# Linear attention with a gated feed-forward: the order of the last block's products and stores, the PSUM pool of kv, the engine of one copy, the place of two weight sums

## The chip, the cores and the metric

The kernel runs on one core of a Trainium2 chip. A core has TensorE (PE: matrix products from SBUF into PSUM, with its weight loads listed apart as PEld), VectorE (DVE), ScalarE (ACT), GpSimd (POOL) and SyncE (SP), each with its own instruction queue worked off in order, and 16 DMA engines that the queues hand transfers to. The metric is the device time of one execution in microseconds (us), as a median over runs.

## The reference, cut to what matters

```python
def _attn_ref(q, k, v):                      # q, k, v: (8 batches, 8 heads, 576 rows, 64)
    q_s = softmax of q over its 64 columns    # exp, then divided by the row's sum
    k_s = softmax of k over its 576 rows      # exp, then divided by the column's sum
    kv = np.einsum('bhsd,bhse->bhde', k_s, v)
    return np.einsum('bhsd,bhde->bhse', q_s, kv)

def _moe_ref(x, w_gate, w_val, w_out):       # x: 4608 x 512; w_gate, w_val: 512 x 1536; w_out: 1536 x 512
    g = x @ w_gate
    gelu = 0.5 * g * (1.0 + erf(g / sqrt(2)))
    return (gelu * (x @ w_val)) @ w_out
```

`x` is the attention output with the heads side by side. The two softmax lines are written in words here; the rest is the reference's. Inputs and output are float32.

## The kernel before, in words

Each batch of 576 rows is cut into 512 main rows (a block) and 64 remaining rows; the 64 remaining rows of all eight batches form a ninth block of 512. The blocks run in the order 0 to 6, then the ninth (called `b == B`), and last batch 7 (L489). Products are in float16 with sums in float32 in PSUM.

One block has these steps, for twelve slices `fi` of 128 hidden columns. `ffn_fi` (L434) makes the gate product `psg` and the value product `psv`, four matmuls each; `gate` (L428) applies Gelu on ACT (`gl`, three buffers) and multiplies on VectorE into `ht`. Blocks 0 and 1 begin with `ffn_first0` and `ffn_first`, which start the products before all four slices of `xt` are there. Block 0 multiplies plainly by `w_out`. All other blocks use `out_strassen` (L550): a Strassen-Winograd form with seven products (`product`, L536) of twelve matmuls of 256 columns each, in place of eight. It needs sums of the weights (`sum_w`, L510: `tw` 1 to 4, made once) and sums of `ht` (`sum_h`, L524: `sh` 1 and 2, `s4`, and one in place). Its PSUM tiles are psa, psb and psc; `snap` copies an intermediate sum to SBUF, `add` adds it to a later one and writes the output tile `yo`.

Attention of later batches rides in between. `exp` (L174) takes exponentials on ACT; `norm` (L218) sums rows of exp(q) on VectorE and multiplies on GpSimd; `unit_td` (L341) transposes exp(q) by one DMA; `unit_kv4` (L294) makes kv from exp(k) and v on TensorE (`pskv`) and divides on VectorE; `unit_x4` (L380) makes x: first the remaining rows (`psxr`, copied to `xtr`), then the main rows (`psx`, copied to `xt`), with one half of the copies on ACT and the other on VectorE. For batch 1, x is made by `unit_x` (L364), one slice of 128 columns at a time, and copied whole by the engine that is named.

What rides where is written out by hand in `plan` (L722 to L778): `at(block, FI, i, ...)` runs the listed steps behind slice i of the block, `at(block, NS, 2 or 4, ...)` behind products 6 and 7 of its Strassen form. The order within each engine's queue is exactly the program's order (`manual_schedule`). The plan's places that the change touches are L741 (third slice of x of batch 1), L754 to L756 (weight sums 2 and 4, and `make_s`, which allocates the `sh` tiles, behind slices 4 to 6 of block 1) and L778 (`unit_kv4` of the next-but-one batch behind `unit_x4`).

PSUM has eight banks. Six are a ring (`big`, L66): a tile takes the tag at the front, which goes to the back at once, or, if held, when it is let go. Two banks are the pool `ps_att`. `bank` (L78) chooses: with `spare` true a tile comes from the ring, else from `ps_att`. `psxr` always takes both banks of `ps_att`; `pskv` of `unit_kv4` takes one of them except after block 3, where `spare` is true. A tile's first matmul waits until the last reader of the bank's earlier tile is done.

The SBUF tiles `yo` hold 256 output rows each, two to a partition: `yo[0]` those of the first half of the block, `yo[1]` those of the second. `store` (L499) issues one DMA to the output; in the last block the rows of `yo[1]` are written in half-rows of 256 columns. In blocks 1 to 6 the products run in the order 1, 2, 5, 6, 3, 7, 4. In the ninth block and the last one (`late`, L589) product 2, which completes the left half of `yo[0]`, comes after product 7:

```python
        late = b == B or last
...
        if last:
            for t in range(2):
                store(nc.sync, yo[1][:, t, c[1]], b, 2 + t, 3 + t, 256, 512)
        if late:
            second()
            store_rows(b, 0, yo[0])
```

In the last block each of psa, psb and psc is two tiles of 128 rows, and product 4 runs by row halves: the first half is copied to `yo[1]` by ACT, the second by VectorE, each followed by its store on SP's queue.

Of the kernel before, what the change touches and what calls it, by code (L numbers as in the profile page):

```python
# [11 lines left out]
ACTF = mybir.ActivationFunctionType  # L12
ALU = mybir.AluOpType

_H_SCALE = 1024.0
# [3 lines left out]
def kernel(  # L19
# [10 lines left out]
    nc = tc.nc  # L30

    B, H, S, D = q.shape
# [33 lines left out]
    def big(shape, dt, name, hold=False):  # L66
        tag = ring.pop(0)
        t = ps_big.tile(shape, dt, name=name, tag=tag)
        if hold:
            held[id(t)] = (t, tag)  # L70
        else:
            ring.append(tag)
        return t

    def let_go(t):
        ring.append(held.pop(id(t))[1])
# [419 lines left out]
    def out_rows(b):  # L496
        return out[b * S:(b + 1) * S, :].rearrange("(m n) c -> m n c", n=NT)

    def store(eng, src, b, n0, n1, c0=0, c1=C):  # L499
        base = out_rows(b)[:, 1 + n0:1 + n1, c0:c1]  # L500
        (pm, nm), (pn, _), _ = base.ap
        last = [[1, (n1 - n0) * C]] if c1 - c0 == C else [[1, c1 - c0]]
        eng.dma_start(out=bass.AP(tensor=base.tensor, offset=base.offset,
                                  ap=[[pm, nm], [NM * pn, 2]] + last), in_=src)
# [31 lines left out]
    def product(i, ps, first, ts=(0, 1)):  # L536
        for j in range(NO):
            for t in ts:
                c0, c1 = slice(t * P, (t + 1) * P), slice(256 + t * P, 256 + (t + 1) * P)
                a = {1: ht[:, j, c0], 2: ht[:, NO + j, c0], 3: s4[:, j, c0], 4: ht[:, NO + j, c1],  # L540
                     5: sh[1][:, j, c0], 6: sh[2][:, j, c0], 7: ht[:, j, c1]}[i]
                w = {1: wo_sb[:, j, 0:256], 2: wo_sb[:, NO + j, 0:256],
                     3: wo_sb[:, NO + j, 256:512]}.get(i)
                if w is None:
                    w = tw[{4: 4, 5: 1, 6: 2, 7: 3}[i]][:, j]
                nc.tensor.matmul(ps[t], a, w, start=(first and j == 0 and (  # L546
                    t == ts[0] or ps[t].tensor is not ps[ts[0]].tensor)),
                                 stop=(j == NO - 1), skip_group_check=True)

    def out_strassen(b, last):  # L550
        yo = [yop.tile([P, 2, C], f32, name="yo", tag="yo") for _ in range(2)]
        c = (slice(0, 256), slice(256, 512))
        ps, tiles_ = {}, {}

        def get(nm):
            if last:
                tiles_[nm] = [big([P, 256], f32, "ps" + nm, True) for _ in range(2)]
                ps[nm] = [x for x in tiles_[nm]]
            else:
                tiles_[nm] = [big([P, 2, 256], f32, "ps" + nm, True)]  # L560
                ps[nm] = [tiles_[nm][0][:, t] for t in range(2)]

        def parts(nm):
            return [(0, ps[nm][0]), (1, ps[nm][1])] if last else [(slice(0, 2), tiles_[nm][0])]

        def snap(nm):
            sn = ffn.tile([P, 2, 256], f32, name="sn", tag="gl")
            for n, (t, src) in enumerate(parts(nm)):
                if n:
                    nc.scalar.activation(out=sn[:, t], in_=src, func=ACTF.Copy, scale=1.0 / _H_SCALE)  # L570
                else:
                    nc.vector.tensor_scalar(out=sn[:, t], in0=src, scalar1=1.0 / _H_SCALE,  # L572
                                            scalar2=None, op0=ALU.mult)
            return sn

        def add(nm, sn, half, col):
            for t, src in parts(nm):
                nc.vector.scalar_tensor_tensor(  # L578
                    out=yo[half][:, t, c[col]], in0=src, scalar=1.0 / _H_SCALE,
                    in1=sn[:, t], op0=ALU.mult, op1=ALU.add)  # L580

        def second():
            get("b")
            product(2, ps["b"], True)
            add("b", s1, 0, 0)
            for x in tiles_["b"]:
                let_go(x)

        late = b == B or last  # L589
        get("a")  # L590
        product(1, ps["a"], True)
        s1 = snap("a")
        if not late:
            second()
        sum_h(NO - 2, NO, (4,))
        get("c")
        product(5, ps["c"], True)
        if not late:
            sum_h(NO - 2, NO, (3,))
        s5 = snap("c")  # L600
        if late:
            sum_h(NO - 2, NO, (3,))
        product(6, ps["a"], False)
        s2 = snap("a")
        ride(b, NS, 2)
        product(3, ps["c"], False)
        add("c", s2, 0, 1)
        for x in tiles_["c"]:
            let_go(x)
        if not late:  # L610
            store_rows(b, 0, yo[0])
        product(7, ps["a"], False)
        add("a", s5, 1, 1)
        ride(b, NS, 4)
        if last:
            for t in range(2):
                store(nc.sync, yo[1][:, t, c[1]], b, 2 + t, 3 + t, 256, 512)
        if late:
            second()
            store_rows(b, 0, yo[0])  # L620
        for ts in ((0,), (1,)) if last else ((0, 1),):
            product(4, ps["a"], False, ts)
            if ts == (1,):
                nc.vector.tensor_scalar(out=yo[1][:, 1, c[0]], in0=ps["a"][1],  # L624
                                        scalar1=1.0 / _H_SCALE, scalar2=None, op0=ALU.mult)
            else:
                t, src = parts("a")[0]
                nc.scalar.activation(out=yo[1][:, t, c[0]], in_=src, func=ACTF.Copy,  # L628
                                     scale=1.0 / _H_SCALE)
            if last:  # L630
                store(nc.sync, yo[1][:, ts[0], c[0]], b, 2 + ts[0], 3 + ts[0], 0, 256)
        for x in tiles_["a"]:
            let_go(x)
        if not last:
            store_rows(b, 1, yo[1])

    def store_rows(b, half, yo):
        if b < B:
            store(nc.sync, yo.rearrange("p n c -> p (n c)"), b, 2 * half, 2 * half + 2)
            return  # L640
        for t in range(2):
            for j in range(2):
                o = 2 * (2 * half + t) + j
                nc.sync.dma_start(
                    out=out[o * S:(o + 1) * S, :].rearrange("(m n) c -> m n c", n=NT)[:, 0, :],
                    in_=yo[j * 64:(j + 1) * 64, t, :])
# [75 lines left out]
    FI, NS = 0, 1  # L722
    plan = {}

    def at(b, kind, i, *fns):
        plan.setdefault((b, kind, i), []).extend(fns)

    L = lambda f, *a: (lambda: f(*a))
# [9 lines left out]
       L(sum_w, 3, "pool"))  # L738
    at(0, NS, 7, L(exp, "q", 2))
    first1 = [[L(unit_t, 1, 1), L(unit_kv, 1, 1)],  # L740
              [L(unit_x, 1, 2, "act"), L(preload, ACTF.Gelu), L(norm, 2, 0, "pool")],  # L741
              [L(unit_x, 1, 3, "dve"), L(norm, 2, 1, "pool")]]

    def x_upper0():
# [5 lines left out]

    at(1, FI, 2, L(unit_trem, 1))
    at(1, FI, 3, L(norm, 2, 2, "pool"), L(load_batch, 3, ((q, "q"), (k, "k"))))
    at(1, FI, 4, L(exp, "k", 2, 0, 4), L(norm, 2, 3, "pool"), make_s)
    at(1, FI, 5, L(sum_w, 2), L(cast_v, 2, 0, H))  # L754
    at(1, FI, 6, L(sum_w, 4))
    at(1, FI, 8, L(exp, "k", 2, 4, 8), L(unit_td, 2))  # L756
    at(1, FI, 11, L(load_batch, 3, ((v, "v"),)), L(exp, "q", 3), L(exp, "k", 3), L(cast_v, 3, 0, H))
    at(1, NS, 2, L(unit_kv4, 2))
# [3 lines left out]
    for b in range(2, B):  # L762
        if b + 2 < B:
            at(b, FI, 0, L(load_batch, b + 2, ((v, "v"), (q, "q"), (k, "k"))))
            at(b, FI, NFI - 1, L(exp, "q", b + 2), L(exp, "k", b + 2), *([exp_rem0] if b == 2 else []))
            vcast = L(cast_v, b + 2, 0, H)
        if b + 1 < B:
            n = b + 1
            for hp in range(HP):
                at(b, FI, hp, L(norm_sum, n, hp), L(norm_mul, n, hp, "pool"))  # L770
            at(b, FI, 4, L(unit_td, n))
            if n + 1 < B:
                at(b, FI, 4, vcast)
            if n == 3:
                at(b, FI, 5, L(unit_kv4, n))
            at(b, NS, 4, L(unit_x4, n, ("act", "dve"), 0 if n == 4 else None))
            if n + 1 < B:
                at(b, NS, 4, L(unit_kv4, n + 1, n == 4))  # L778


    def ride(b, kind, i):
        for fn in plan.get((b, kind, i), []):
            fn()
# [62 lines left out]
```

## Time and profile before

| | us |
|---|---|
| median of 4 runs (306.85 to 307.12) | 307.02 |
| the profiled execution | 307.08 |
| its span, first to last instruction | 305.3 |
| TensorE busy (96% of the span) | 293.8 |
| VectorE busy (66%) | 201.6 |
| ACT busy (48%) | 145.9 |
| GpSimd busy (27%) | 81.6 |
| last matmul issued, its products ended | 301.15 |
| last output store issued | 301.8 |

The time of an execution is the span and 1.78 us around it. The profile has one row for each instruction or run of equal instructions; in the timeline's rows the columns are start and duration in us, engine, line of the kernel, operation, the tile written and the tiles read, their shapes, and how many instructions the row joins. In square brackets stands how long the engine had been idle ahead of it and, as far as semaphores show it, what ended the wait. SPq rows are DMA issues on SP's queue: their duration is the issuing, not the transfer. The chain of waits is followed back from the last instruction: at each step to what released it.

### The profile page before, as it was taken

The page shows a single profiled execution, that of the slowest core. Times are in us where ns is not written, and L with a number is a line of the kernel's source. Part 1 is how long each engine was busy: PE and PEld are TensorE (multiplying, and loading weights), DVE is VectorE, ACT ScalarE, POOL GpSimd, SP SyncE. Part 2 cuts the span into 40 slices and gives each one's busy share as a digit, 9 for nine tenths or more (in the row PEclk, how much of TensorE's full clock was granted, in tenths as well). Part 3 has the DMA queues.
Part 4 walks back from the last instruction along what each step waited for, and adds up shares of the span by engine and source line. Part 5 has one row for each costly group of instructions (what it writes and reads, how often), then busy time and mean ns, then how long its engine had stood idle before and what let it go on. Part 6 is the DMA issues. An engine that isn't in the chain of part 4 may idle for free.

```text
span 305.3 us, 5368 instructions
## 1 busy us (share of the span) xinstructions
PE 293.8 (96%) x2077; PEld 167.5 (55%) x2077; DVE 201.6 (66%) x390; ACT 145.9 (48%) x195; POOL 81.6 (27%) x85
## 2 busy tenths in 40 slices
PE   3999999998999999999999999999999999999994
PEld 1544445445744575448544854486447644764473
DVE  2944377868866875877677758674867536834672
ACT  4763477789352574346633853385331333123320
POOL 2667568763036001800081007200600000000000
PEclk9999999999999999999999999999999999999999
DMA  7999999995189115950597049603040300032003
GB/s 230 372 383 392 400 388 385 328 304 159 71 257 322 44 45 194 375 85 2 188 382 120 1 153 378 160 0 140 0 86 3 124 16 0 0 79 60 1 2 137
DMA packets 54761, 51.66 MB, mean 169 GB/s; under 512 B 18512, under 2 KB 50768, under 8 KB 54736
## 3 DMA queue, kind: packets, MB, share of 16 engines
q1 hardware_dynamic: 53152, 49.75, 51.4%
q10 hardware_dynamic: 1584, 1.57, 1.6%
q8 instruction: 16, 0.26, 0.3%
q14 instruction: 9, 0.07, 0.1%
HBM read 37.75 MB, written 9.44 MB: 155 GB/s over the span
## 4 chain that ended last, share of the span: by engine, by line
PE 73%; DVE 0%; ACT 0%; issue 0%
PE psg L425 24%; PE psv L425 24%; PE psa L546 14%; PE psc L546 6%; PE psb L546 3%; PE pskv L301 2%; PE psx L388 1%; PE psxr L388 0%; DVE yo L578 0%; ACT xt L156 0%; DVE yo L624 0%; ACT xtr L156 0%; PE psxr L398 0%
## 5 line engine op out<-in xcount | busy, mean ns | idle before, releaser
L431 DVE SCALAR_TENSOR_TENSOR ht<-psv,gl 128x512 f16<-128x512 f32 x108 | 73.7, 685 | 66.4 <-PE psv L425 46.8
L430 ACT ACTIVATE gl<-psg 128x512 f32<-128x512 f32 x108 | 63.2, 597 | 95.6 <-PE psg L425 95.2
L425 PE MATMUL psg<-xt,wg_sb 128*128 128x512 f16 x384 | 100.5, 379 | 0.2 <-ACT xt L156 0.2
L425 PE MATMUL psv<-xt,wv_sb 128*128 128x512 f16 x384 | 100.5, 379 | 0.0
L425 PEld LDWEIGHTS <-wv_sb 128*128 128x128 f16 x432 | 42.2, 98 | 51.2 <-issue 0.7
L425 PEld LDWEIGHTS <-wg_sb 128*128 128x128 f16 x432 | 42.1, 98 | 48.7
L215 POOL TENSOR_TENSOR eq<-eq,rrq 128x640 f16<-128x640 f16 (+1 forms) x27 | 34.4, 1274 | 119.8 <-issue 103.0
L546 PEld LDWEIGHTS <-ht 128*128 128x128 f16 x384 | 37.1, 98 | 7.6 <-issue 0.8
L196 DVE TENSOR_REDUCE rq<-eq 128x10 f32<-128x640 f16 x28 | 22.7, 810 | 3.0 <-ACT eq L178 3.0
L546 PE MATMUL psa<-tw,ht 128*128 128x256 f16 x192 | 23.6, 273 | 0.2 <-DVE yo L578 0.2
L154 POOL CAST v<-vt 128x640 f16<-128x640 f32 x26 | 19.2, 781 | 9.4 <-DMA vt<-in_v_dram 9.4
L178 ACT ACTIVATE ek<-kt 128x1280 f16<-128x1280 f32 (+1 forms) x11 | 19.1, 1746 | 3.4 <-DMA kt<-in_k_dram 3.4
L546 PEld LDWEIGHTS <-sh 128*128 128x128 f16 x192 | 18.8, 98 | 3.1 <-issue 0.9
L178 ACT ACTIVATE eq<-qt 128x2560 f16<-128x2560 f32 (+2 forms) x10 | 18.5, 1864 | 2.5 <-DMA qt<-in_q_dram 2.5
L628 ACT ACTIVATE yo<-psa 128x512 f32<-128x512 f32 (+1 forms) x8 | 4.6, 570 | 20.4 <-PE psa L546 20.4
L572 DVE TENSOR_SCALAR sn<-psa 128x512 f32<-128x512 f32 (+1 forms) x16 | 10.4, 653 | 3.8 <-PE psa L546 3.8
L156 ACT CAST xtr<-psxr 128x128 f16<-128x128 f32 (+1 forms) x8 | 2.1, 290 | 22.1 <-PE psxr L388 15.1
L546 PE MATMUL psa<-tw,sh 128*128 128x256 f16 x96 | 11.8, 272 | 0.7 <-DVE sn L572 0.7
L425 PE MATMUL psg<-xtr,wg_sb 128*128 128x512 f16 x48 | 12.3, 379 | 0.0
L425 PE MATMUL psv<-xtr,wv_sb 128*128 128x512 f16 x48 | 12.3, 379 | 0.0
L546 PE MATMUL psb<-wo_sb,ht 128*128 128x256 f16 x96 | 12.0, 273 | 0.2 <-DVE ht L431 0.2
L546 PE MATMUL psc<-wo_sb,s 128*128 128x256 f16 x96 | 11.8, 273 | 0.0
(86 smaller groups left out, 265.3 us busy)
## 6 DMA issues: line engine op xcount, KB each, us to landing
out_dram<-yo SPq DMA_DIRECT2D x15, 512.0 KB, 3.3
kt<-in_k_dram SPq DMA_DIRECT2D x7, 640.0 KB, 8.5
vt<-in_v_dram SPq DMA_DIRECT2D x7, 640.0 KB, 5.0
qt<-in_q_dram SPq DMA_DIRECT2D x7, 640.0 KB, 6.8
qt<-in_q_dram SPq DMA_DIRECT2D x8, 512.0 KB, 7.4
wost<-in_moe_w_out_dram SPq DMA_DIRECT2D x6, 512.0 KB, 7.9
kt<-in_k_dram SPq DMA_DIRECT2D x6, 512.0 KB, 9.7
vt<-in_v_dram SPq DMA_DIRECT2D x6, 512.0 KB, 5.6
```

The lines of the kernel that those rows point to most:

```text
L154: nc.gpsimd.tensor_copy(out=dst, in_=src)
L178: nc.scalar.activation(out=dst[:, n0:NC, h0 * D:h1 * D].rearrange(o, d=D, **({"t": 2} if b >= QUAD else {})), in_=heads(tiles[(nm, b)], b, ...
L196: nc.vector.reduce_sum(rq, e, axis=mybir.AxisListType.X)
L215: (nc.gpsimd if eng == "pool" else nc.vector).tensor_tensor(out=e, in0=e, in1=rrq.unsqueeze(-1).to_broadcast((P, n, 2, D)), op=ALU.mult)
L301: nc.tensor.matmul(ps[s * D:(s + 1) * D, hp, :], ek_b[b % 2][:, n, c0:c0 + D], v16_b[b % 2][:, n, 2 * hp + s, 0:VW], start=(n == 0), stop= ...
L388: nc.tensor.matmul(ps[s][64 * t:64 * t + 64], st[(b, "kv4")][r, hp, :], src[r], start=True, stop=True)
L425: nc.tensor.matmul(ps, w[:, ci, fi * P:(fi + 1) * P], xt[:, ci, :], start=(ci == 0), stop=(ci == HP - 1))
L430: nc.scalar.activation(out=gl, in_=psg, func=ACTF.Gelu)
L431: nc.vector.scalar_tensor_tensor(out=ht[:, fi, :], in0=psv, scalar=_H_SCALE, in1=gl, op0=ALU.mult, op1=ALU.mult)
L546: nc.tensor.matmul(ps[t], a, w, start=(first and j == 0 and (t == ts[0] or ps[t].tensor is not ps[ts[0]].tensor)), stop=(j == NO - 1), ski ...
L572: nc.vector.tensor_scalar(out=sn[:, t], in0=src, scalar1=1.0 / _H_SCALE, scalar2=None, op0=ALU.mult)
L628: nc.scalar.activation(out=yo[1][:, t, c[0]], in_=src, func=ACTF.Copy, scale=1.0 / _H_SCALE)
```

## The change

The last block takes the order of blocks 1 to 6 up to product 3, so that `yo[0]` is complete and its 512 KB are stored (SP) ahead of products 7 and 4. These two run by row halves in a new function `finish_last`; one 128 KB half-row store goes out on ACT's queue, and two stores (256 KB and 128 KB) on SP's queue follow. `unit_kv4` behind `unit_x4` always takes its bank from the ring: after blocks 2, 4 and 5 too, not only after 3. The copy of the third x slice of batch 1 goes from ACT to VectorE, ahead of a norm sum. Weight sums 2 and 4 both run behind slice 4 of block 1, ahead of `make_s`, and not behind slices 5 and 6.

```diff
@@ out_strassen
-        late = b == B or last
+        late = b == B
...
         if not late:
             store_rows(b, 0, yo[0])
+        if last:
+            finish_last(b, ps["a"], yo[1], s5)
+            return
         product(7, ps["a"], False)
         add("a", s5, 1, 1)
         ride(b, NS, 4)
-        if last:
-            for t in range(2):
-                store(nc.sync, yo[1][:, t, c[1]], b, 2 + t, 3 + t, 256, 512)
         if late:
             second()
             store_rows(b, 0, yo[0])
-        for ts in ((0,), (1,)) if last else ((0, 1),):
-            product(4, ps["a"], False, ts)
-            if ts == (1,):
-                nc.vector.tensor_scalar(out=yo[1][:, 1, c[0]], in0=ps["a"][1],
-                                        scalar1=1.0 / _H_SCALE, scalar2=None, op0=ALU.mult)
-            else:
-                t, src = parts("a")[0]
-                nc.scalar.activation(out=yo[1][:, t, c[0]], in_=src, func=ACTF.Copy,
-                                     scale=1.0 / _H_SCALE)
-            if last:
-                store(nc.sync, yo[1][:, ts[0], c[0]], b, 2 + ts[0], 3 + ts[0], 0, 256)
-        for x in tiles_["a"]:
-            let_go(x)
-        if not last:
-            store_rows(b, 1, yo[1])
+        product(4, ps["a"], False)
+        nc.scalar.activation(out=yo[1][:, :, c[0]], in_=tiles_["a"][0], func=ACTF.Copy,
+                             scale=1.0 / _H_SCALE)
+        let_go(tiles_["a"][0])
+        store_rows(b, 1, yo[1])
+
+    def finish_last(b, ps, yo, s5):
+        for t in range(2):
+            product(7, ps, False, (t,))
+            nc.vector.scalar_tensor_tensor(
+                out=yo[:, t, 256:], in0=ps[t], scalar=1.0 / _H_SCALE, in1=s5[:, t],
+                op0=ALU.mult, op1=ALU.add)
+        store(nc.scalar, yo[:, 1, 256:], b, 3, 4, 256, 512)
+        product(4, ps, False, (0,))
+        nc.scalar.activation(out=yo[:, 0, 0:256], in_=ps[0], func=ACTF.Copy, scale=1.0 / _H_SCALE)
+        store(nc.sync, yo[:, 0], b, 2, 3)
+        product(4, ps, False, (1,))
+        nc.vector.tensor_scalar(out=yo[:, 1, 0:256], in0=ps[1], scalar1=1.0 / _H_SCALE,
+                                scalar2=None, op0=ALU.mult)
+        store(nc.sync, yo[:, 1, 0:256], b, 3, 4, 0, 256)
@@ plan
-              [L(unit_x, 1, 2, "act"), L(preload, ACTF.Gelu), L(norm, 2, 0, "pool")],
+              [L(unit_x, 1, 2, "dve"), L(preload, ACTF.Gelu), L(norm, 2, 0, "pool")],
...
-    at(1, FI, 4, L(exp, "k", 2, 0, 4), L(norm, 2, 3, "pool"), make_s)
-    at(1, FI, 5, L(sum_w, 2), L(cast_v, 2, 0, H))
-    at(1, FI, 6, L(sum_w, 4))
+    at(1, FI, 4, L(exp, "k", 2, 0, 4), L(norm, 2, 3, "pool"), L(sum_w, 2), L(sum_w, 4), make_s)
+    at(1, FI, 5, L(cast_v, 2, 0, H))
...
-                at(b, NS, 4, L(unit_kv4, n + 1, n == 4))
+                at(b, NS, 4, L(unit_kv4, n + 1, True))
```

## The prediction

> **What bounds the kernel now.** I read the page's totals first, then the chain that ended last, then the timeline at the places that the diff touches.
>
> ```profile
> PE 293.8 (96%) x2077; PEld 167.5 (55%) x2077; DVE 201.6 (66%) x390; ACT 145.9 (48%) x195; POOL 81.6 (27%) x85
> ...
> PE 73%; DVE 0%; ACT 0%; issue 0%
> ```
>
> TensorE is busy for 96% of the span, and the chain hardly leaves it. So an edit is worth what it takes out of TensorE's few gaps, plus what it does to the tail, where TensorE has ended (301.15 us) and only stores are left. The granted clock is 1.000, so no throttle is to be gained or lost. I work on the profiled execution: 307.08 us, a span of 305.3 us and 1.78 us around it; it lies 0.06 us above the median of 307.02.
>
> **Part 1: kv in the large pool.** After batches 2, 4 and 5 the sums pskv of the next-but-one batch move from the small PSUM pool (two banks) to the ring of six. After batch 3 they are there already, so the trace has both forms. Timeline at the end of batch 2:
>
> ```profile
> 113.01 0.61 PE L388 MATMUL psx<-eqt,kv 64*64 64x512 f16 x8
> 113.22 0.27 ACT L156 CAST xtr<-psxr 128x128 f16<-128x128 f32 x1 [1.92 <-PE psxr L388]
> 113.44 1.07 ACT L156 CAST xt<-psx 128x512 f16<-128x512 f32 x2
> 113.64 0.28 DVE L158 CAST xtr<-psxr 128x128 f16<-128x128 f32 x1
> ...
> 114.04 0.74 PEld L301 LDWEIGHTS <-ek 128*64 128x64 f16 x40 [0.91 <-ACT xt L156]
> 114.07 0.82 PE L301 MATMUL pskv<-v,ek 128*64 128x65 f16 x40 [0.45 <-ACT xt L156]
> ```
>
> The profile blames ACT's xt copy. In the built program the wait is on VectorE's xtr copy (113.64 + 0.28 = 113.92), whose bank pskv takes over; VectorE is late because it adds psa first. Now the ends of batch 3 (large pool) and of batch 4 (small pool):
>
> ```profile
> 145.03 0.60 PE L388 MATMUL psx<-eqt,kv 64*64 64x512 f16 x6
> ...
> 145.56 0.82 PE L301 MATMUL pskv<-v,ek 128*64 128x65 f16 x40
> ```
>
> ```profile
> 176.40 0.60 PE L388 MATMUL psx<-eqt,kv 64*64 64x512 f16 x8
> ...
> 176.93 0.71 PEld L301 LDWEIGHTS <-ek 128*64 128x64 f16 x40 [0.41 <-ACT xtr L156]
> 176.93 0.82 PE L301 MATMUL pskv<-v,ek 128*64 128x65 f16 x40
> ```
>
> From the last run of psx to pskv it is 0.53 us in both, and 1.06 us in batch 2. After batch 4 pskv inherits the bank that ACT frees (176.61 + 0.27 = 176.88), just in time; batch 5 stands likewise (207.77 to 208.30). So the gain is **1.06 - 0.53 = 0.53 us once**, and nothing after 4 and 5. In the built program the new bank after batch 2 was last read by the add of psc (ended 112.41), so it is free. What is late next: TensorE reaches the next gate product at 115.61 instead of 116.14; its xt copies end at 115.12 on VectorE. Margin 0.49 us, so it holds. The bank's next user is the third gate product of the next batch (117.34 at the earliest); the kv product on VectorE that frees it ends at 115.66. Bounds: 0.40 to 0.55.
>
> **Part 2: third x of batch 1 on VectorE.**
>
> ```profile
> 52.36 0.57 ACT L156 CAST xt<-psx 128x512 f16<-128x512 f32 x1
> ...
> 52.97 0.38 PE L425 MATMUL psg<-xt,wg_sb 128*128 128x512 f16 x1 [0.22 <-ACT xt L156]
> ...
> 53.47 0.63 DVE L158 CAST xt<-psx 128x512 f16<-128x512 f32 x1
> ...
> 54.27 0.38 PE L425 MATMUL psg<-xt,wg_sb 128*128 128x512 f16 x1
> ```
>
> ACT copies the third x at 52.36, after a 2.34 us exponential. Its product started at 51.29 and VectorE is idle from 51.47 to 52.48, so there the copy runs from about 51.74 to 52.37, and the reduce behind it, which waits for the same exponential (52.45), is not delayed. TensorE can go on at 52.37 + 0.215 (the pitch of these products) = 52.585 instead of 52.97: 0.385. But six products later it needs the fourth x, still copied from 53.47 to 54.10 behind that reduce. With 0.05 us for the signal (as 76.30 to 76.35 below) the product of 54.27 can start at 54.15. So **0.12 us** is left; bounds 0 and 0.385.
>
> **Part 3: the two weight sums go before the sixth gate.** They cost 1.07 and 0.94 us of VectorE (64.08 and 65.67). Behind the last norm sum VectorE is idle from 60.95 to 63.47, waiting for ACT, so they end at 62.97, ahead of the ht product queued behind them. That makes VectorE earlier only until 70.38, where it again waits for ACT's tenth Gelu (0.97 us). That Gelu hangs on ACT's chain of table loads, not on VectorE, so the TensorE stall on the twelfth ht (0.53 + 0.25 us of waits at 73.91) stays. What they do meet is GpSimd:
>
> ```profile
> 73.84 3.10 POOL L154 CAST v<-vt 128x640 f16<-128x640 f32 x4 [8.11 <-DMA vt<-in_v_dram]
> 73.89 0.95 DVE L532 TENSOR_TENSOR sh<-ht 128x512 f16<-128x512 f16 x1
> ...
> 74.87 0.82 DVE L532 TENSOR_TENSOR sh<-sh,ht 128x512 f16<-128x512 f16 x1
> 75.62 0.68 DVE L572 TENSOR_SCALAR sn<-psa 128x512 f32<-128x512 f32 x1
> 76.35 1.47 PE L546 MATMUL psa<-tw,sh 128*128 128x256 f16 x12 [0.74 <-DVE sn L572]
> ```
>
> These two sums have a median of 0.425 us; beside the cast they lost 0.53 + 0.40 = 0.93 us, and TensorE waits 0.74 us at 76.35. The other way round, the fourth cast at 64.29, started during the weight sum of 64.08 to 65.15, took 1.44 us instead of 0.72. So the moved sums will hold back the norm product on GpSimd (61.10, 1.26 us) by up to about 0.95 us, the rest of the first sum. Behind it on SP's queue stand the transpose (62.38, 5.10 us, waits for that product) and then the load of v (67.58) that releases the cast of 73.84: all later by as much. The sh sums then run free, and product 6 may start up to 0.9 us sooner. But then the cast, from 74.8 to 77.9, meets the next pair (s and ht, at 76.0 and 76.4), which the copy of psc waits for. With 0.93 us lost there, product 3 starts at 78.2 to 78.4 against 78.50. Bounds: 0.3 lost (three sums hit) to 0.8 gained (none hit). I take **0.13**, near the lower half, because the cast is moved and not removed.
>
> The rule that speaks against this part is in the Trainium skill, SBUF — State Buffer, section "Who interferes with whom": a VectorE operation with two SBUF inputs and a GpSimd operation that reads SBUF exclude each other, and whichever starts first holds the port for its whole instruction. Taken strictly it would let the norm product in between the two sums, and VectorE's next ht would start some 0.8 us late; the rows of 64.29 and 73.89 agree with it, and by it part 3 would stand at its low end, 0.3 us lost, if it went on blocking each pair in turn. From the rows alone: that ht may start up to 1.6 us late before anything feels it (0.5 us of idle, then 1.1 us until the Gelu of 65.26 wants its buffer), so I charge nothing.
>
> **Part 4: the end.** TensorE has the same 84 products in the last block and ends at 301.15 as before. Product 2 moves up behind product 1 and needs the twelfth ht (292.78) only for its last two pairs; the two sums before product 3 end by about 296.2, product 3 starts at 297.06. Product 7 by halves ends its first half at 299.03; its add runs 299.24 to 299.62, just before product 4 wants the bank (299.68). Before:
>
> ```profile
> 298.91 3.59 SPq L503 DMA_DIRECT2D out_dram<-yo  x5
> ...
> 300.53 0.38 ACT L628 ACTIVATE yo<-psa 128x256 f32<-128x256 f32 x1 [4.20 <-PE psa L546]
> 301.19 0.42 DVE L624 TENSOR_SCALAR yo<-psa 128x256 f32<-128x256 f32 x1 [0.66 <-PE psa L546]
> ```
>
> The five stores go out at 298.91, 299.5, 300.55 (512 KB), 301.18 and 301.8; by the DMA view they land after 2.1, 2.1, 3.0, 2.7 and 2.4 us, the last at 304.2, and 1.1 us later the span ends. From 301.75 to 303.75 the DMA engines are full: that is what stretches 2.1 to 2.4. After: 512 KB leaves at 299.29 (adds end at 299.22) and is gone by 302. The half row block goes out on ACT's queue at 300.22; its issue holds ACT (issues there took 0.65 to 0.72 us at the kernel's start), so the copy queued behind it starts at 300.90 instead of 300.53 and ends at 301.28. SP waits for it: 256 KB at 301.35 to 301.92, the last 128 KB at 301.82 to 301.95. Landing after 2.1 to 2.4 us gives 303.92 to 304.35 against 304.2: between 0.28 gained and 0.15 lost. I take **0.10 gained**, because the queue is emptier. Cover gone would mean a longer issue on ACT; see rival C.
>
> **Sum.** 0.53 + 0.12 + 0.13 + 0.10 = 0.88 us: 307.08 - 0.88 = **306.2 us**, 0.29% faster. About 0.2%, 0.61 us, is what a measurement of this kernel can tell from no change.
>
> **Rivals.**
> A, *only kv pays*: fourth x, cast and stores take everything else back. For it: each of the other parts runs into a next wait named above. 307.08 - 0.53 = 306.55, no difference that counts.
> B, *the cast slips past both pairs of sums*: parts 1, 2 and 4 give 0.75, part 3 its full 0.8: 305.5. Against it: the cast lasts 3.1 us and the sums stand 2 us apart.
> C, *slower: the store on ACT holds the last copy*. With an issue of length i the last store leaves at 300.22 + i + 0.38 + 0.06 + 0.61. The longest issue of an output store in this trace is 1.60 us: the last store then leaves at 302.87 and lands 2.4 to 3.0 us later (3.0 is the longest of the five), 1.07 to 1.67 later than now. With nothing from parts 2 and 3: 307.08 - 0.53 + 1.07 to 1.67 = 307.6 to 308.2, say 307.9. The kernel is slower than before from about i = 1.2 on (301.27 + 1.2 + 2.25 = 304.72, 0.52 late). Against it: the last five stores took 0.54 to 0.67 to issue.
> D, *the kv gain doesn't come*: another bank's wait stands in its place, the rest as forecast: 306.73.
>
> **Chances.** Forecast 0.54, A 0.24, B 0.13, C 0.05, D 0.04. Faster by over 0.2%: forecast and B, with a little of A's upper edge, 0.68; within: 0.27; slower: 0.05. The range 305.4 to 306.8 leaves out C, some of B and the worst of parts 3 and 4.
>
> **What would show it.** Batch 2's pskv 0.53 us behind its psx run; the product now at 54.27 about 0.1 us earlier; the norm product of 61.10 longer or later, the cast of 73.84 later, and the sh sums at 0.42 us; the last store issued near 301.9 less what came before. It is wrong if the cast stays beside the sh sums, if batch 3's first gate product waits for xt, or if the issue on ACT takes over 1 us.

## The result, and the profile after

| | before | after |
|---|---|---|
| median, us | 307.11 (76 runs) | 306.63 (51 runs) |
| profiled execution, us | 307.08 | 306.62 |
| its span, us | 305.3 | 304.8 |
| TensorE's last product ends, us | 301.15 | 300.59 |

The ratio is 0.9981, with a 95% interval from 0.9974 to 0.9987. The kernel is faster by 0.48 us, 0.16% by the medians: the forecast sign, inside the forecast range, but about half of the 0.88 us that were forecast, and just inside the 0.2% that the prediction called no change that can be told, although the interval leaves out 1. Rival A (306.55, only kv pays) is the nearest case. (The 76 runs of before include its runs beside the change; the prediction knew only 307.02.)

The totals and the chain of the page of after, against those of before:

```profile
PE 293.4 (96%) x2077; PEld 167.3 (55%) x2077; DVE 203.7 (67%) x391; ACT 145.5 (48%) x194; POOL 82.5 (27%) x85
...
PE 73%; DVE 1%; issue 0%
```

The same 2077 products take TensorE the same time. VectorE is busy 2.1 us longer and GpSimd 0.9 us, though only one copy moved to VectorE (0.69 us). Part of the rest is instructions that take longer: the two weight sums alone are busy 2.89 us where they took 1.07 + 0.94.

**End of batch 2, kv.** Timeline of after:

```profile
112.95 0.60 PE L388 MATMUL psx<-eqt,kv 64*64 64x512 f16 x8
112.97 0.69 DVE L578 SCALAR_TENSOR_TENSOR yo<-psa,sn 128x512 f32<-128x512 f32 x1 [0.62 <-PE psa L546]
113.17 0.27 ACT L156 CAST xtr<-psxr 128x128 f16<-128x128 f32 x1 [1.92 <-PE psxr L388]
113.38 1.07 ACT L156 CAST xt<-psx 128x512 f16<-128x512 f32 x2
...
113.48 0.82 PE L301 MATMUL pskv<-v,ek 128*64 128x65 f16 x40
113.58 0.28 DVE L158 CAST xtr<-psxr 128x128 f16<-128x128 f32 x1
...
115.56 0.81 PE L425 MATMUL psg<-xt,wg_sb 128*128 128x512 f16 x3
```

pskv now starts 0.53 us behind psx, and no longer 1.06. It starts before VectorE's xtr copy (113.58), so that copy's bank is not what it waits for any more. TensorE was 0.06 us ahead of the trace of before when this stretch began (112.95 against 113.01) and is 0.58 ahead at the next gate product (115.56 against 116.14), which starts without a wait.

**Third x of batch 1:**

```profile
50.34 2.34 ACT L178 ACTIVATE eq<-qt 128x2560 f16<-128x2560 f32 x1 [0.98 <-DMA qt<-in_q_dram]
...
51.73 0.69 DVE L158 CAST xt<-psx 128x512 f16<-128x512 f32 x1 [0.24 <-PE psx L367]
...
52.71 0.82 DVE L196 TENSOR_REDUCE rq<-eq 128x10 f32<-128x640 f16 x1 [0.29 <-ACT eq L178]
...
53.70 0.63 DVE L158 CAST xt<-psx 128x512 f16<-128x512 f32 x1
...
54.38 0.38 PE L425 MATMUL psg<-xt,wg_sb 128*128 128x512 f16 x1 [0.31 <-DVE xt L158]
```

The third copy sits where it was forecast (51.74), and the wait has moved to the fourth x, as forecast. But that product starts at 54.38, later than the 54.27 of before. Read upwards: fourth copy, norm sum, and the exponential, which started at 50.34 where it had 50.11 in the trace of before, because the load of q that it waits for landed 0.23 us later.

**The weight sums and the cast.** First the norm product, the transpose and the load of v before:

```profile
61.10 1.26 POOL L215 TENSOR_TENSOR eq<-eq,rrq 128x640 f16<-128x640 f16 x1 [0.40 <-DVE rrq L198]
...
62.38 5.10 SPq L344 DMA_TRANSPOSE eqt<-eq  x1
...
67.58 1.29 SPq L134 DMA_DIRECT2D vt<-in_v_dram  x2
```

Then after: where the sums went, and where the cast of batch 3's v meets the sums of block 1:

```profile
61.02 2.89 DVE L515 TENSOR_TENSOR tw<-wo_sb,tw 128x1536 f16<-128x1536 f16 x2
61.21 1.89 POOL L215 TENSOR_TENSOR eq<-eq,rrq 128x640 f16<-128x640 f16 x1 [0.40 <-DVE rrq L198]
...
63.12 4.39 SPq L344 DMA_TRANSPOSE eqt<-eq  x1
63.84 1.87 DVE L431 SCALAR_TENSOR_TENSOR ht<-psv,gl 128x512 f16<-128x512 f32 x3
...
67.61 1.29 SPq L134 DMA_DIRECT2D vt<-in_v_dram  x2
```

```profile
74.00 0.42 DVE L532 TENSOR_TENSOR sh<-ht 128x512 f16<-128x512 f16 x1
...
74.04 3.16 POOL L154 CAST v<-vt 128x640 f16<-128x640 f32 x4 [7.29 <-DMA vt<-in_v_dram]
...
74.46 0.82 DVE L532 TENSOR_TENSOR sh<-sh,ht 128x512 f16<-128x512 f16 x1
...
75.94 1.47 PE L546 MATMUL psa<-tw,sh 128*128 128x256 f16 x12 [0.21 <-DVE sn L572]
...
76.58 0.89 DVE L532 TENSOR_TENSOR s<-ht,sh 128x512 f16<-128x512 f16 x1
...
78.46 0.70 PE L546 MATMUL psc<-wo_sb,s 128*128 128x256 f16 x5 [0.30 <-DVE sn L572]
```

The norm product takes 1.89 us instead of 1.26, and the transpose is issued 0.74 us later (63.12 against 62.38). But its issue takes 4.39 us instead of 5.10, and the load of v behind it starts at 67.61 against 67.58: the lateness ends on SP's queue. The cast is 0.20 us late and not 0.7, and only 0.03 of that come from the queue: from the load's issue to the cast it is 6.43 us instead of 6.26 (6.12 to 6.57 in the other traces that have the cast at this place). That is enough to let the first sh sum start ahead of it; product 6 is 0.41 us earlier, the sum s pays (0.89 us instead of 0.42), and product 3 comes at 78.46 against 78.50.

**The end:**

```profile
297.79 2.80 PE L546 MATMUL psa<-tw,ht 128*128 128x256 f16 x24
...
298.66 3.52 SPq L503 DMA_DIRECT2D out_dram<-yo  x3
299.30 0.42 DVE L630 SCALAR_TENSOR_TENSOR yo<-psa,sn 128x256 f32<-128x256 f32 x1 [0.23 <-PE psa L546]
299.75 0.60 ACTq L503 DMA_DIRECT2D out_dram<-yo  x1
300.56 0.38 ACT L635 ACTIVATE yo<-psa 128x256 f32<-128x256 f32 x1 [3.50 <-PE psa L546]
300.63 0.42 DVE L638 TENSOR_SCALAR yo<-psa 128x256 f32<-128x256 f32 x1 [0.91 <-PE psa L546]
```

SP's stores are issued at 298.66, 300.96 and 301.63; by the DMA view the last lands after 2.1 us, at about 303.7. From TensorE's end to the end of the profiled execution it was 307.08 - 301.15 = 5.93 us; it is 306.62 - 300.59 = 6.03. The new tail loses 0.10 us.

So the account of the change is: 0.06 us ahead before kv, 0.52 from kv, 0.02 given up after it, hence 0.56 at TensorE's end; less 0.10 in the tail is 0.46 = 307.08 - 306.62.

### The profile page after: what moved, and what is told of

The parts are those of the page before. It is cut to its first block, busy times and chain, and to the rows that moved or that the text cites. A ratio compares the mean times of both kernels' runs of the same rounds, so it can differ in the third digit from the quotient of the medians.

```text
span 304.8 us, 5370 instructions
## 1 busy us (share of the span) xinstructions
PE 293.4 (96%) x2077; PEld 167.3 (55%) x2077; DVE 203.7 (67%) x391; ACT 145.5 (48%) x194; POOL 82.5 (27%) x85
## 4 chain that ended last, share of the span: by engine, by line
PE 73%; DVE 1%; issue 0%
PE psg L425 24%; PE psv L425 24%; PE psa L546 13%; PE psc L546 6%; PE psb L546 3%; PE pskv L301 1%; PE psx L388 1%; DVE yo L578 0%; PE psxr L388 0%; DVE s L532 0%; DVE sn L572 0%; DVE yo L638 0%; DVE ht L532 0%; PE psxr L398 0%
## 5 line engine op out<-in xcount | busy, mean ns | idle before, releaser
L546 PE MATMUL psa<-wo_sb,ht 128*128 128x256 f16 x96 | 11.8, 273 | 0.0
```

What stands on the lines that cost most here:

```text
L546: nc.tensor.matmul(ps[t], a, w, start=(first and j == 0 and (t == ts[0] or ps[t].tensor is not ps[ts[0]].tensor)), stop=(j == NO - 1), ski ...
```

## The experiments

My theory after the result: kv pays its 0.53 us and nothing else does; the third x is worth its 0.12 but hidden by a late load; the place of the weight sums is worth nothing, because sums and cast collide wherever they stand; the store on ACT's queue costs what the new order of the tail gains. Rivals: the parts pay but the tail costs more than it seems; or the moved sums are what delays things.

| kernel | us | ratio to before, 95% |
|---|---|---|
| kv_only | 306.63 | 0.9978 (0.9969 to 0.9987) |
| all_but_kv | 307.30 | 0.9996 (0.9983 to 1.001) |
| old_tail | 306.52 | 0.9978 (0.9968 to 0.9987) |
| store_on_sp | 306.15 | 0.9963 (0.9951 to 0.9976) |
| x_on_act | 306.84 | 0.9984 (0.9975 to 0.9993) |
| sums_back | 306.65 | 0.9983 (0.9974 to 0.9992) |
| x4_first | 306.32 | 0.9972 (0.9961 to 0.9983) |
| v_late | 305.88 | 0.9957 (0.9943 to 0.9971) |
| x_only | 307.05 | 0.9996 (0.9988 to 1.0005) |
| three_mends | 305.03 | 0.9930 (0.9917 to 0.9944) |
| four_mends | 304.61 | 0.9915 (0.9901 to 0.9928) |
| before_again | 307.13 | one execution |

### kv alone, and everything but kv

kv_only is before with one line changed, all_but_kv is after with that line as it was:

```diff
-                at(b, NS, 4, L(unit_kv4, n + 1, n == 4))
+                at(b, NS, 4, L(unit_kv4, n + 1, True))
```

> The kernel before with the large pool for kv after blocks 2, 4 and 5, and nothing else of the change. Theory: the kv edit is the whole gain. pskv of block 2 starts 0.53 us behind its last run of psx, the span is 0.5 us shorter than before's 305.3, the time 306.6 us, ratio 0.9983, like the whole change. Rival (the gain is spread over the parts): 306.85 us, ratio 0.9991.

> The whole change except the kv edit (the pool choice is as before). Theory: nothing is left, 307.1 us, ratio 1.000 (between 0.9995 and 1.0005), the last block about 0.06 us earlier than before and the tail giving it back. Rival (the gain is spread): 306.8 us, ratio 0.999.

Measured: 306.63 and 307.30, each beside a before of 307.28. kv alone is worth 0.65 us by the medians; the rest together can't be told from nothing (0.9996, from 0.9983 to 1.001). In the trace of kv_only psx starts at 112.85 and pskv at 113.39 (0.54); in all_but_kv 112.90 and 113.96 (1.06). Rival A of the prediction, that only kv pays, holds for the whole.

### The tail: old order, and the store on SP

old_tail is after with the last block's code of before. store_on_sp is after with this:

```diff
-        store(nc.scalar, yo[:, 1, 256:], b, 3, 4, 256, 512)
+        store(nc.sync, yo[:, 1, 256:], b, 3, 4, 256, 512)
```

> The change with the last block as it was before. Theory: the new tail costs about 0.1 us, so this is 0.1 us faster than the whole change: 306.5 us, the last store issued 0.65 us after TensorE's end and landing 2.4 us later. Rival (the new tail pays because its DMA queue is emptier): 0.1 to 0.3 us slower than the whole change, 306.75 to 306.9 us.

> The change with the half-row store of the last block on SP's queue instead of ACT's. Theory: ACT is free for the last copy, which starts about 0.1 us after its product ends (0.6 us earlier against the last block's first product than in the change), the last store is issued 0.65 us or less after TensorE's end instead of 1.04 and still lands about 2.1 to 2.3 us later: 0.3 to 0.5 us faster than the change, 306.2 to 306.3 us. Rival (the transfers themselves set the end): the stores come closer together, the last one lands 2.5 us or more after its issue, and the time is the change's 306.6 us.

Measured: 306.52, as forecast, and 306.15, just below the forecast. The timeline of store_on_sp:

```profile
297.97 2.80 PE L546 MATMUL psa<-tw,ht 128*128 128x256 f16 x24
...
298.84 2.97 SPq L503 DMA_DIRECT2D out_dram<-yo  x4
299.48 0.42 DVE L630 SCALAR_TENSOR_TENSOR yo<-psa,sn 128x256 f32<-128x256 f32 x1 [0.23 <-PE psa L546]
300.15 0.38 ACT L635 ACTIVATE yo<-psa 128x256 f32<-128x256 f32 x1 [2.91 <-PE psa L546]
```

Its TensorE runs 0.18 us later than that of after (297.97 against 297.79), yet ACT's copy starts at 300.15 against 300.56: measured from TensorE, 0.59 us earlier. The last store goes out at 301.26 against 301.63, 0.55 us earlier by the same measure. What held ACT in after is its own queue. The view of line L635 of after (durations in ns as least, median and most, then the first and last start in us):

```profile
L635 ACTq EVENT_SEMAPHORE  x2: 38/38/38, 300.4 to 300.5; - x2
L635 ACT ACTIVATE yo<-psa x1: 383/383/383, 300.6 to 300.6; 128x256 f32<-128x256 f32 x1
```

The issue holds ACT from 299.75 to 300.35, two semaphore instructions follow, and the copy starts only at 300.56, though the views name psa as its releaser. So the new order is worth about 0.37 us against the old tail when SP issues all stores (306.15 against 306.52), and 0.11 us less than nothing when ACT issues one. The second difference is inside the intervals; the traces put it at 0.10 as well (from TensorE's end to the end of the execution 5.93 us in old_tail, 6.03 in after). In store_on_sp it is 5.48 us: the last store goes out 0.49 us after TensorE's end (0.65 before) and lands after 2.1 us (2.4 before). So the rival of store_on_sp, that the transfers set the end, is out. That the last 0.21 us (300.35 to 300.56) are those two waits is read from the rows, not tested by itself. The Trainium skill, DMA: Bandwidth & Descriptors, section "Issuing engines are not separate DMA queues", says that issuing from several engines saves only the sequencer's time for the issue, usually small beside the transfer; here that time, 0.60 us, was taken from the engine that had the critical copy behind it.

### Third x: back to ACT, alone, and the fourth x first

x_on_act is after with the third x on ACT again; x_only is before with the third x on VectorE; x4_first is after with the norm sum behind the fourth x:

```diff
-              [L(unit_x, 1, 2, "dve"), L(preload, ACTF.Gelu), L(norm, 2, 0, "pool")],
-              [L(unit_x, 1, 3, "dve"), L(norm, 2, 1, "pool")]]
+              [L(unit_x, 1, 2, "dve"), L(preload, ACTF.Gelu)],
+              [L(unit_x, 1, 3, "dve"), L(norm, 2, 0, "pool"), L(norm, 2, 1, "pool")]]
```

> The change with the third x of batch 1 copied on ACT again. Theory: the fourth x sets the end of this stretch in both forms (its copy stands behind a norm sum that waits for an exponential), so the product that needs it starts at 54.3 us here as at 54.38 in the change: 306.6 us, within 0.1 us of the change. Rival (the third x holds TensorE for 0.385 us): 307.0 us, the product at 54.7.

> The kernel before with the third x of batch 1 copied on VectorE, and nothing else. Theory: TensorE gains 0.12 us at the product that needs the fourth x, measured against the end of the exponential that the copy stands behind (which follows the load of q and was at 52.45 us in one trace of before and up to 52.69 in others): that product starts 1.70 us behind the exponential's end instead of 1.82; 307.1 us, within 0.15 of before. Rival (the copy itself is worth its 0.385 us): 306.8 us.

> The change with the norm sum of batch 2 moved behind the copy of the fourth x on VectorE. Theory: the fourth x is there at about 53.3 us, its product starts at 53.9 instead of 54.38, and TensorE is 0.45 us earlier up to product 6 of that block; there the cast of v takes part of it back, so 0.1 to 0.45 us faster: 306.2 to 306.5 us. Rival (the first Gelu waits for its table load, or the cast takes back all): 306.6 us.

> The kernel before once more, for a second trace. Theory: the start of the exponential of batch 2's q follows the load stream and varies by some 0.2 us from execution to execution of one kernel; here anywhere from 50.1 to 50.4. Rival (something in the change shifts it by 0.2 us): 50.1 again. The rest as in the first trace: span 305.2 to 305.5 us.

Measured: 306.84, 307.05 and 306.32. x_on_act is 0.21 us above after, where at most 0.1 was forecast; x_only is 0.14 below its before (307.19). That is the direction of the move, but not to be told from nothing by these intervals. The traces tell it, if the exponential's end is the zero point. To the product that needs the fourth x it is 1.70 us with the move (after 52.68 to 54.38; x_only 52.65 to 54.35) and 1.81 or 1.82 without (before 52.45 to 54.27; before_again 52.63 to 54.44; x_on_act 52.68 to 54.50). The move is worth **0.12 us**, as forecast. (In x_on_act's trace another 0.08 us go at the sums of block 1, see the table below.) The exponential itself starts at 50.11 in the first trace of before and at 50.29 in before_again, the same program; with the move it starts at 50.34 in after and at 50.11 in four_mends below. So the 0.23 us that hid the gain need no edit to explain them: on the page of after the DMA engines are full there (387 and 388 GB/s in the two slices from 38 to 53 us), and the load lands a little sooner or later from one execution to the next. Timeline of x4_first, the third and the fourth copy:

```profile
51.85 0.69 DVE L158 CAST xt<-psx 128x512 f16<-128x512 f32 x1 [0.24 <-PE psx L367]
...
52.93 0.69 DVE L158 CAST xt<-psx 128x512 f16<-128x512 f32 x1 [0.39 <-PE psx L367]
```

With the fourth copy ahead of the sum it no longer waits for the exponential: the product that needs it starts at 54.03 instead of 54.38, and the output products of block 2 start 0.35 us earlier than in after (104.56 against 104.91). That is the gain that the forecast saw at the third x (0.385) and lost at the fourth.

### The sums back, and the cast away

sums_back is after with the weight sums at their old places. v_late moves the load and the cast of batch 3's v behind the sums of block 1:

```diff
-    at(1, FI, 11, L(load_batch, 3, ((v, "v"),)), L(exp, "q", 3), L(exp, "k", 3), L(cast_v, 3, 0, H))
+    at(1, FI, 11, L(exp, "q", 3), L(exp, "k", 3))
...
-    at(1, NS, 4, L(unit_x4, 2, ("act", "dve"), 1))
+    at(1, NS, 4, L(unit_x4, 2, ("act", "dve"), 1), L(load_batch, 3, ((v, "v"),)), L(cast_v, 3, 0, H))
```

> The change with the two weight sums where they were before. Theory: their place is worth nothing, because SP's transpose issue gets shorter by what it starts later (4.4 instead of 5.1 us) and the load of v leaves at 67.6 us either way; whether the cast starts just ahead of the sh sums or just behind them is chance, and product 3 starts at 78.3 to 78.6 in all cases: 306.6 us, within 0.15 of the change. Rival (the place is what gained): the sh sums take 0.95 and 0.82 us again, product 3 starts 0.2 us or more later than 78.46, 306.8 us or more.

> The change with load and cast of batch 3's v put behind block 1's stores, so that GpSimd is idle while VectorE makes the last sums of block 1. Theory: the sums take 0.42 us each, product 6 starts at about 75.5 and product 3 at 77.5 to 77.7 instead of 78.46, and the cast, now at 87 to 91 us, is done before kv of batch 3 wants it at 93.8: 0.7 to 0.9 us faster, 305.75 to 305.95 us. Rival 1 (something else than GpSimd made these sums slow): the sums stay at 0.8 to 0.95 us and the time at 306.6. Rival 2 (the cast now meets block 2's norm products and kv of batch 3 waits for it): product 3 is early, kv of batch 3 late, 306.4 us or more.

Measured: 306.65 and 305.88. The same three places in each trace, as start of the cast, start of the first sh sum, length of the two sh sums and of s, and time from the start of the first sh sum to product 3 (us):

| kernel | cast | sh | sh, sh, s | to product 3 |
|---|---|---|---|---|
| before | 73.84 | 73.89 | 0.95, 0.82, 0.42 | 4.61 |
| before_again | 73.90 | 74.07 | 0.83, 0.82, 0.41 | 4.49 |
| kv_only | 73.69 | 73.92 | 0.76, 0.82, 0.41 | 4.43 |
| x_only | 74.18 | 73.98 | 0.42, 0.82, 0.89 | 4.46 |
| sums_back | 74.07 | 73.92 | 0.43, 0.82, 0.89 | 4.46 |
| after | 74.04 | 74.00 | 0.42, 0.82, 0.89 | 4.46 |
| x_on_act | 74.01 | 74.13 | 0.88, 0.82, 0.41 | 4.54 |
| store_on_sp | 73.97 | 74.02 | 0.94, 0.82, 0.42 | 4.61 |
| v_late | 87.52 | 74.00 | 0.42, 0.42, 0.41 | 3.72 |

The pattern does not follow the place of the weight sums: sums_back and x_only have them where before has them, and look like after; x_on_act and store_on_sp have them moved, and look like before. It follows which of the two, cast or first sh sum, starts first, by 0.04 to 0.23 us. The cast waits for the load of v, and that varies by more than this margin, as said above. (all_but_kv, old_tail and x4_first stand as after does.) Either way two sums lose time, and product 3 comes 0.71 to 0.89 us later than in the last row. The timeline of v_late shows the price with the cast gone:

```profile
74.00 0.42 DVE L532 TENSOR_TENSOR sh<-ht 128x512 f16<-128x512 f16 x1
...
74.46 0.42 DVE L532 TENSOR_TENSOR sh<-sh,ht 128x512 f16<-128x512 f16 x1
...
75.56 1.47 PE L546 MATMUL psa<-tw,sh 128*128 128x256 f16 x12
...
76.18 0.41 DVE L532 TENSOR_TENSOR s<-ht,sh 128x512 f16<-128x512 f16 x1
...
77.72 1.48 PE L546 MATMUL psc<-wo_sb,s 128*128 128x256 f16 x12
```

All sums take 0.41 or 0.42 us, products 6 and 3 start without a wait, and product 3 is 0.74 us earlier than in after: so much was the collision worth. The kernel is 0.75 us faster than the change. Rival 2 is out too: kv of batch 3 starts at 93.06, 0.73 us earlier than in after. What the move costs shows one block later, where the next cast now meets block 2's first sh sum (0.88 us instead of 0.43); TensorE does not lose by it (its last 24 products start 0.73 us earlier than in after).

### What was left: together, and one wait more

three_mends is after with store_on_sp, x4_first and v_late. four_mends also moves the second half of k's exponential up to the first, so that ACT changes its tables twice less (16 table loads instead of 18, 1283 ns each):

```diff
-    at(1, FI, 4, L(exp, "k", 2, 0, 4), L(norm, 2, 3, "pool"), L(sum_w, 2), L(sum_w, 4), make_s)
+    at(1, FI, 4, L(exp, "k", 2, 0, 4), L(exp, "k", 2, 4, 8), L(norm, 2, 3, "pool"), L(sum_w, 2), L(sum_w, 4), make_s)
...
-    at(1, FI, 8, L(exp, "k", 2, 4, 8), L(unit_td, 2))
+    at(1, FI, 8, L(unit_td, 2))
```

> The change with three edits of the earlier runs together: the half-row store on SP's queue, the norm sum behind the copy of the fourth x, load and cast of batch 3's v behind block 1's stores. Theory: they act at three separate places and add up, 0.3 + 0.75 + 0.45 us: 305.1 us, ratio 0.9935 to before. Rival (the earlier TensorE runs into loads that have not come): 305.4 us or more.

> The three edits, and both halves of batch 2's exponential of k behind slice 4 of block 1, so that ACT changes its table twice less. Theory: the twelfth ht of block 1 is done at about 71.4 us instead of 73.6, product 2 does not wait for it (0.78 us), 304.3 to 304.5 us. Rival (the second half, now at 61.5 to 62.8, holds the sixth Gelu and through it TensorE): 305.1 us or more.

Measured: 305.03 and 304.61. Against after's ratio the three mends gain 0.18%, 0.09% and 0.24% alone, 0.51% in sum, and 0.51% together: they don't meet. The stall in before (three_mends has the same rows 0.15 us earlier), where product 2 stops for the twelfth ht:

```profile
72.41 1.25 PE L546 MATMUL psb<-wo_sb,ht 128*128 128x256 f16 x10
...
73.91 0.11 PEld L546 LDWEIGHTS <-ht 128*128 128x128 f16 x2 [0.53 <-DVE ht L431]
73.91 0.39 PE L546 MATMUL psb<-wo_sb,ht 128*128 128x256 f16 x2 [0.25 <-DVE ht L431]
...
74.14 1.47 PE L546 MATMUL psc<-tw,sh 128*128 128x256 f16 x12
```

Timeline of four_mends:

```profile
59.82 2.43 ACT L178 ACTIVATE ek<-kt 128x1280 f16<-128x1280 f32 x2
...
70.98 0.68 DVE L431 SCALAR_TENSOR_TENSOR ht<-psv,gl 128x512 f16<-128x512 f32 x1
...
71.97 1.47 PE L546 MATMUL psb<-wo_sb,ht 128*128 128x256 f16 x12
...
73.28 1.47 PE L546 MATMUL psc<-tw,sh 128*128 128x256 f16 x12
```

The twelfth ht, at 73.02 in three_mends, comes at 70.98, and product 2 runs whole instead of stopping for its last two matmuls, the stall that the prediction left standing. Product 3 starts at 76.75 against 77.46, but 0.25 us of these 0.71 are the zero point again (the exponential of q starts at 50.11 here and at 50.36 in three_mends). From the start of product 2 to that of the next product it is 1.31 us here and 1.73 in three_mends as in before. So the stall was worth 0.42 us, and by the medians the kernel gains 0.42. The forecast, 304.3 to 304.5, is missed because it took the waits of 0.53 and 0.25 us as 0.78: they stand in the rows of the weight load and of the product, which overlap, and are one stall seen twice. four_mends is the best version here, 0.85% faster than before and 0.66% faster than the change (0.9915 against 0.9981).

## Why the prediction was right or wrong

**What bounds the kernel: right.** TensorE keeps its products and its 96%; every gain came out of its gaps or the tail.

**Part 1, kv: right** (0.53 forecast, 0.52 in the traces of after and of kv_only, 0.65 by the medians of kv_only). The wait was on VectorE's xtr copy, as the built program said and the profile did not. Nothing came after batches 4 and 5: the lead is 0.57 to 0.59 us from there to the last block (291.24 against 291.81).

**Part 2, third x: right in mechanism and size** (0.12), measured from the exponential. What the forecast had not allowed for is that this zero point itself moves by up to 0.25 us between traces (50.11 to 50.36), twice the gain. Why the load lands when it does was not pursued.

**Part 3, weight sums: the number came out, the step failed.** From 0.11 us late at 54.38 to 0.04 early at product 3 is 0.15 us, against 0.13 forecast. But sums_back gets the same with the sums at their old place, so the move is worth nothing that the runs can tell. The step that failed is "all later by as much": 0.74 us of lateness at the transpose became 0.03 at the load of v. The norm product ends 0.74 us later, 0.63 of it by its own length (up to 0.95 forecast). Of the two victims only one changed: the first sh sum goes free and s pays, while the second sh sum still takes 0.82 us, where the forecast had both sh sums free. The cast stays beside the sh sums, and that is a sign that the prediction itself had named for being wrong. So the 0.15 us are luck. I took the cast's start as something that the edit sets; it is a race, decided by 0.04 to 0.23 us in the table above, which either side wins for nearly the same price. The rule of the Trainium skill, SBUF — State Buffer, section "Who interferes with whom", had the direction, not the size: VectorE's next ht starts at 63.84 against 63.47, 0.37 us late (0.11 of it brought along from the late load) and not 0.8, and nothing felt it. The stall on the twelfth ht stayed, as forecast, but it was never 0.53 + 0.25 us: four_mends puts it at 0.42.

**Part 4, the tail: wrong sign, inside its bounds.** Forecast 0.10 gained (bounds 0.28 gained to 0.15 lost), measured 0.10 lost. The mis-sized term is "the copy queued behind it starts at 300.90": less the 0.57 us that TensorE was ahead that is 300.33, and it was 300.56. The issue took 0.60 us, within 0.1 of the forecast; it started 0.10 us later, and 0.21 us of waits stood between it and the copy. The last store left at 301.63 where 301.25 to 301.38 was forecast, and landed after 2.1 us, the short end. Rival C had the mechanism, at a price that did not come (an issue of 1.2 us or more).

**The sum.** 0.88 forecast; 0.46 came. The missing 0.42 us are 0.20 in the tail, 0.19 in parts 2 and 3 (0.25 forecast, 0.06 left at kv, the late load of 0.23 taking most of it), and 0.03 at kv and behind it. Rival A's reason, that each other part runs into a next wait, is what the runs show for the tail and the sums; the third x paid its 0.12 us, and a later load hid it.

## What to carry to other kernels

A wait on a PSUM bank can be taken at its price when another batch of the same kernel already runs without it: that row is the forecast. A store given to a second engine's queue costs that engine its issue time and the waits behind it, so give it to one that has nothing critical queued. Where two instructions block each other, moving a neighbour only changes which of them loses; move one of the two out of the other's stretch, and look for the stretch by asking when its result is needed (v was first read at 93.79, 16.6 us after its cast had ended, in after).

## What the runs showed of the hardware

- The transpose's issue on SP has no fixed length. Batch 2's starts between 62.38 and 63.25 us in the 14 traces, takes 4.29 to 5.21, and ends between 67.30 and 67.75 wherever it started (5.10 from 62.38 in before, 4.39 from 63.12 in after). Batch 3's takes 4.60 us in after and 8.52 in v_late, where the loads ahead of it are issued from 90.26 to 94.94 and not from 85.29 to 90.36. So a delay ahead of it need not reach what stands behind it; what sets its end was not pursued.
- The blocking between VectorE's sums of two SBUF operands and GpSimd goes both ways. Undisturbed, the four casts of v take 721 ns each (v_late); beside the sums of block 1 they take 717 to 972 ns (after). The two weight sums took 0.96 and 1.89 us beside the norm product, which took 1.89 instead of 1.26.
- The same program's exponential, fed by a load, started 0.18 us apart in two executions (50.11, 50.29) whose times differ by 0.05 us: a single trace can't price an edit of 0.1 us there without a zero point of its own.
- The idle time in brackets is not what a stall costs TensorE: at the twelfth ht of block 1 the product's row says 0.25 us, and from start to start 0.42 us were lost.
